# A TensorE-bound kernel in 66 steps: a new instruction list, an output half cut in two, and one weight piece fewer kept in memory

## The chip, the cores and the metric

One NeuronCore of a Trainium2 chip. The metric is the device time of one execution, in microseconds (us), median of the runs. The kernel before takes 3138.72 us (three runs, 3137.41 to 3142.72). The same kernel differs between chips (3133.5 to 3142.3 us for the kernel before, medians of five sets of runs; the later four are from chips 15, 8, 14 and 10), so an experiment is always compared with runs of the kernel before on its own chip.

## The reference

```python
def _A_ref(x, mem0, Wq, Wk, Wv, Wo, seg_len):      # 64 segments of 32 rows, 32 heads of 192
    ...
    for s in range(n_seg):
        xs = x[:, s * seg_len:(s + 1) * seg_len, :].copy()
        h = jnp.concatenate([mem, xs], axis=1)           # 8 memory rows + 32 rows
        q = jnp.einsum('btd,dhe->bhte', h, Wq)           # k and v alike
        ...
        o = jnp.einsum('bhte,hed->btd', o, Wo)
        mem = o[:, :M, :].copy()                         # the next segment needs this one
        outs.append(o[:, M:, :])
def _B_ref(x, wqkv, wo):  # local dilated attention, 32 heads of 20
    ...
x = A_x
x = x + _A_ref(_layernorm(x), A_mem0, A_Wq, A_Wk, A_Wv, A_Wo, A_seg_len)
x = x + _B_ref(_layernorm(x), B_wqkv, B_wo)
x = x + _A_ref(_layernorm(x), A_mem0, A_Wq, A_Wk, A_Wv, A_Wo, A_seg_len)   # same weights again
x = x + _B_ref(_layernorm(x), B_wqkv, B_wo)
```

(Defaults cut.) The width is 640, and layer A's projections are 640 x 6144, so A's weights are 31.5 MB; the kernel keeps only a part of them on the core. The memory rows make layer A a recurrence over 64 segments.

## The kernel before

The kernel runs a segment of the first layer pair and a segment of the second, two segments behind, as two lanes of 40 columns in the same matmuls. That makes 66 steps for A; 62 of them have both lanes (I call them full steps), the first two and the last two have one. After the last there is one more step of B alone.

In each step all of A's weights are used once. They are cut into 128 pieces of eight or seven 128x128 blocks ("long", 256 KB, and "short", 224 KB). Some pieces are resident (loaded once and kept in the core's memory); the others are streamed in every step through a ring of eight slots:

```python
RING = 8
N_RES = 79
PIECE = (8, 7)
...
def load_piece(self, u):
    ...
    res = u in self.resident
    if res:
        t_ = self.wres.tile([P, w], BF16, name="w_{}{}_{}{}".format(*u))
    else:
        t_ = self.wring.tile([P, P * PIECE[0]], BF16, name="w_ring")
    ...
    self.nc.sync.dma_start(out=t_[:, 0:w], in_=src)
```

The order of all instructions of a step is one hand-set list. Heads are handled in eight "quads". For quad i, Ki, Qi, Vi are projections (30 matmuls each); KEi, QEi, VEi copy them out of PSUM, the memory that matmuls write to (KE, VE on ScalarE, QE on VectorE); Ti, TEi transpose V and copy it; Si are the scores, Ei the exponentials (ScalarE), EMi the mask (VectorE); POi is probabilities times V; Ri the reciprocal of the sums (three ScalarE instructions); OT1i, OT2i the normalised outputs (VectorE, three instructions); Oai, Obi the two halves of the output projection, 15 matmuls each. LSQ, lst, LMV, LR, LAP are the layer norm of the next step, MEMa and MEMb copy the new memory rows into the next step's input, X1 adds the residual. Small letters are layer B. The end of the list before:

```
... OT24 VE6 Ob1 E6 QE7 PO5 T6 EM6 TE6 by byE R5 K7 KE7 V7 S7 VE7 OT15 E7 OT25 LSQ PO6 EM7 Oa2 R6 T7 Ob2 Oa3 TE7
Ob3 OT16 OT26 Oa5 PO7 Oa6 R7 lst LMV Ob5 Oa4 Ob6 OT17 LR OT27 Ob4 LAP O7x O7y MEMa O7z MEMb X1
```

Each engine gets its own instructions in this order, and the timelines below show them in it. There is one buffer for PO's result, so PO7 waits for OT26.

The softmax here doesn't subtract the row's maximum and nothing guards it: scores larger than these inputs give would overflow.

Of the kernel before, what the change touches and what calls it, by code (L numbers as in the profile page):

```python
# [21 lines left out]
NQUAD = 8  # L22
# [13 lines left out]
BDIL = 2  # L36

RING = 8
N_RES = 79
PIECE = (8, 7)  # L40
O_ROWS = ((0, 2, 3), (5, 1, 4))

# [2 lines left out]


ORDER = """
K0 Q0 bsq K0y QE0 KE0 V0 bst bmv VE0 Q1 S0 K1 T0 QE1 br bap E0 TE0 KE1 V1 S1 EM0 Q3 PO0 VE1 QE3 E1 bq T1 R0 K2
KE2 bqE TE1 Q2 K3 V2 QE2 OT10 S2 KE3 bk EM1 OT20 S3 PO1 VE2 E2 bkE Q4 T2 EM2 bs1 E3 QE4 V3 R1 K4 TE2 be1 VE3
Q5 OT11 OT21 KE4 PO2 R2 EM3 T3 eb1 bs0 be0 V4 QE5 Oa0 VE4 bv TE3 OT12 OT22 bvE Q6 S4 PO3 eb0 E4 bt R3 QE6 btE  # L50
K5 T4 EM4 K6 KE5 TE4 bp0 V5 OT13 Ob0 OT23 KE6 on0 S5 bp1 VE5 PO4 T5 Oa1 E5 R4 on1 TE5 V6 bo Q7 EM5 OT14 S6 boE
OT24 VE6 Ob1 E6 QE7 PO5 T6 EM6 TE6 by byE R5 K7 KE7 V7 S7 VE7 OT15 E7 OT25 LSQ PO6 EM7 Oa2 R6 T7 Ob2 Oa3 TE7
Ob3 OT16 OT26 Oa5 PO7 Oa6 R7 lst LMV Ob5 Oa4 Ob6 OT17 LR OT27 Ob4 LAP O7x O7y MEMa O7z MEMb X1
""".split()


# [4 lines left out]
def half_order():  # L61

    order = []
    for n in ORDER:
        if n[0] in "KQV" and len(n) == 2:
            order += [(n[0].lower(), int(n[1]), 0), (n[0].lower(), int(n[1]), 1)]
        elif n[:2] in ("Oa", "Ob"):
            order.append(("o", int(n[2]), int(n[1] == "b")))
        elif n == "O7x":
            order += [("o", 7, 0), ("o", 7, 1)]  # L70
    assert len(set(order)) == len(order) == 8 * NQUAD
    return order

def half_blocks(kind, i, h):

    if kind == "o":
        if i == NQUAD - 1:
            blocks = [(m, c) for c in range(NC) for m in O_ROWS[0] + O_ROWS[1]]
        else:
            blocks = [(m, c) for rows in O_ROWS for m in rows for c in range(NC)]  # L80
    elif (kind, i) == ("k", 0):
        blocks = [(c, n) for c in range(NC - 1) for n in range(6)] + [(NC - 1, n) for n in range(6)]
    else:
        blocks = [(c, n) for n in range(6) for c in range(NC)]
    return blocks[15 * h:15 * (h + 1)]


NO_WEIGHTS = {"T": 4, "S": 3, "PO": 3, "bst": 3, "lst": 3, "bq": 10, "bk": 10, "bv": 8, "bt": 3, "bo": 2, "by": 8, "bp": 2, "bs": 8}

def resident_pieces():  # L90

    at, t = {}, 0.0
    for n in ORDER:
        if n[0] in "KQV" and len(n) == 2 and n != "K0":
            at.update({(n[0].lower(), int(n[1]), h): t + 15 * h for h in range(2)})
        elif n == "K0":
            at.update({("k", 0, h): t + 15 * h for h in range(2)})
        elif n[:2] in ("Oa", "Ob"):
            at[("o", int(n[2]), int(n[1] == "b"))] = t
        elif n == "O7x":  # L100
            at.update({("o", 7, h): t + 15 * h for h in range(2)})
        t += 30 if len(n) == 2 and n[0] in "KQV" else 15 if n[0] == "O" and n[1] in "ab" else 30 if n == "O7x" else NO_WEIGHTS.get(n.rstrip("01234567"), 0)
    pieces = [(at[u] + 8 * q, u + (q,)) for u in half_order() for q in range(2)]
    pieces.sort()
    stream, n_s = set(), len(pieces) - N_RES
    k = 0
    for j in range(n_s):
        want = (j + 0.5) * t / n_s
        while k < len(pieces) - (n_s - j) and abs(pieces[k + 1][0] - want) <= abs(pieces[k][0] - want):
            k += 1  # L110
        stream.add(pieces[k][1])
        k += 1
    return {u for _, u in pieces} - stream

class Kernel:
    def __init__(self, ctx, tc, xT, m0T, wA, wqkv, wo, out):

        self.tc = tc
        self.nc = tc.nc
        self.x = xT  # L120
        self.mem0 = m0T
        self.wA = wA
        self.b_src = (wqkv, wo)
        self.out = out
        self.n_seg = 2 * xT.shape[0]
        pool = lambda name, bufs, **kw: ctx.enter_context(tc.tile_pool(name=name, bufs=bufs, **kw))
        self.cp = pool("consts", 1)
        self.wres = pool("wres", 1)
        self.wring = pool("wring", RING)
        self.ap1 = pool("act1", 1)  # L130
        self.ap2 = pool("act2", 2)
        self.bp = pool("bact", 1)
        self.xp = pool("xio", 1)
        self.ps_one = pool("ps_one", 1, space=PSUM)
        self.units = {}
        self.place = {u: n for n, u in enumerate(half_order())}
        self.resident = resident_pieces()
        self.cur = {}
        self.n_big = 0
        self.xt, self.ots, self.qxs, self.kp, self.qp, self.vp, self.tp = {}, {}, {}, {}, {}, {}, {}  # L140
        self.x_load(0)
        self.build_consts()
# [154 lines left out]
    def proj(self, ps, kind, i, h, t, chained=False):  # L297

        hT = self.hT[t % 2]
        c0, c1 = self.cs.start, self.cs.stop  # L300
        for k, (c, n) in enumerate(half_blocks(kind, i, h)):
            yield k
            self.nc.tensor.matmul(ps[:, NT * n + c0:NT * n + c1], lhsT=self.block(kind, i, h, k), rhs=hT[:, NT * c + c0:NT * c + c1],  # L303
                                  start=(h == 0 and k == 0) if chained else c == 0, stop=(c == NC - 1), skip_group_check=chained)
# [111 lines left out]
    def o_mm(self, i, h, k, first=False):  # L416
        m, c = half_blocks("o", i, h)[k]
        ot = self.ots[i][:].rearrange("p a b n -> p (a b) n")
        o = NT * (c % 3) + self.cs.start
        self.nc.tensor.matmul(self.acc[c // 3][:, o:o + self.cs.stop - self.cs.start], lhsT=self.block("o", i, h, k), rhs=ot[:, m, self.cs],  # L420
                              start=first, stop=False, skip_group_check=True)
# [8 lines left out]
    def a_o7(self, part):  # L430

        for k in {"x": range(18), "y": range(18, 24), "z": range(24, 30)}[part]:
            self.o_mm(NQUAD - 1, k // 15, k % 15)

    def acc_lanes(self, g):

        return self.acc[g][:, 0:(3 - g) * NT].rearrange("p (c l n) -> p c l n", l=2, n=LT)
# [301 lines left out]
    def a_piece(self, n, t):  # L739
        if n == "K0":  # L740
            return self.k0(t)
        if n == "K0y":
            return self.k0y()
        if n[:2] == "O7":
            return self.a_o7(n[2])
        if n == "X1":
            return self.b_x1(t)
        k, i = n[:-1], int(n[-1])
        if k == "K":
            self.kp[i] = self.proj6("k", i, t)  # L750
        elif k == "Q":
            self.qp[i] = self.proj6("q", i, t)
        elif k == "V":
            self.vp[i] = self.proj6("v", i, t)
        elif k in ("Oa", "Ob"):
            self.a_o(i, int(k == "Ob"))
        else:
            {"KE": self.kE, "QE": self.qE, "VE": self.vE, "T": self.a_t, "TE": self.tE, "S": self.a_s, "E": self.sE, "EM": self.sM,
             "R": self.dR, "PO": self.a_pv, "OT1": self.ot1, "OT2": self.ot2}[k](i)
# [51 lines left out]
def laid_out(A_x, A_mem0, A_Wq, A_Wk, A_Wv, A_Wo, B_wqkv, B_wo):  # L811

    chunks = lambda a: a.reshape(a.shape[0], NC, P, -1).transpose(0, 2, 1, 3).reshape(a.shape[0], P, -1)
    x = A_x[0]
    xT = x.reshape(x.shape[0] // NX, NX, D).transpose(0, 2, 1)
    w = {k: a.reshape(D, NQUAD, QE).transpose(1, 0, 2) for k, a in (("k", A_Wk), ("q", A_Wq), ("v", A_Wv))}
    w["o"] = A_Wo.reshape(NQUAD, QE, D)

    def half(k, i, h):
        b = w[k][i].reshape(-1, P, w[k].shape[2] // P, P)  # L820
        b = np.stack([b[r, :, c] for r, c in half_blocks(k, i, h)], 1)
        return np.concatenate([b[:, :PIECE[0]].ravel(), b[:, PIECE[0]:].ravel()])

    wA = np.stack([half(*u) for u in half_order()])
    wo = B_wo.reshape(BH // 2, 2, BD, D).transpose(1, 0, 2, 3).reshape(2, D // 2, D)
    wo = np.stack([wo[0, 0:P], wo[1, 192:], wo[0, P:256], wo[1, 64:192], np.concatenate([wo[0, 256:], wo[1, 0:64]])], 1).reshape(P, -1)
    out = {"xT": chunks(xT), "m0T": chunks(A_mem0[0].T[None])[0], "wA": wA, "wqkv": chunks(B_wqkv.reshape(D, 3, D).transpose(1, 0, 2)), "wo": wo}
    return {k: np.ascontiguousarray(v) for k, v in out.items()}
# [24 lines left out]
```

## Time and profile before

| | before |
|---|---|
| median | 3138.72 us |
| TensorE busy | 98% of the span |
| bound of a full step by its matmuls alone, my estimate from their start-to-start times | 46.2 us |
| undisturbed full step (the shortest of 62) | 46.43 us |
| mean full step | 46.62 us |
| streamed per step | 49 pieces, 11,808 KB |

From the page of the kernel before: the busy times; two lines of its DMA queues (packets, MB, share of 16 engines); and the engines' shares of the chain that ended last (the waits followed back from the last instruction of the kernel).

```profile
PE 3063.2 (98%) x83160; PEld 3036.4 (97%) x83160; DVE 2358.2 (75%) x6883; ACT 1747.2 (56%) x3829; POOL 48.2 (2%) x162
...
q1 hardware_dynamic: 477648, 820.89, 83.2%
q8 instruction: 651, 10.67, 1.4%
...
PE 95%; DMA 3%; issue 1%; DVE 1%; ACT 0%; SPq 0%; DVEq 0%; ACTq 0%
```

TensorE (PE), with 95% of that chain, is the bound: everything else matters only where it makes TensorE wait, or sets when it may go on. The second queue: 651 packets of 16,384 B. TensorE has 83,160 weight loads and as many matmuls, 166,320 instructions; with the 475 others of its trace that is 651 blocks of 256, so I take these packets for TensorE's own instructions. The profile counts them on the same 16 DMA engines as the weights (1.4% of the span, the weights' queue 83.2%).

What fills a full step is best read from the starts of matmuls. In this trace a pair of weight load and 80-column matmul takes 35.7 ns, a 128-column one 56 ns, start to start. The following lines are from the timeline of TensorE in the kernel before, in the last 9 us of a full step; columns are start, duration, engine, line, operation, tiles, shape, count. The lines are, in order: end of V7, PO6, PO7, the last seven blocks of the output projection, and the first blocks of K0 of the next step.

```profile
1529.37 0.42 PE L303 MATMUL ps_v<-hT_92,w_v_11_1654 128*128 128x80 bf16 x7
...
1529.90 0.45 PE L401 MATMUL ps_o<-Em,Vt_134 80*128 80x80 bf16 x8
...
1533.25 0.46 PE L401 MATMUL ps_o<-Em,Vt_134 80*128 80x80 bf16 x8
...
1537.17 0.42 PE L420 MATMUL ps_acc_51496<-OT,w_o_11_1962 128*128 128x80 bf16 x7
1537.61 0.45 PE L303 MATMUL ps_k<-hT_90,w_k_00_386 128*128 128x80 bf16 x8
```

A group of seven issues in 7 x 35.7 = 250 ns (the printed duration contains the modelled end of the last one). So the last group is issued by 1537.42, and K0 starts at 1537.61: TensorE waits 0.19 us. That is the "hand-over" wait, found in nearly every full step. Before PO7 there is another, 0.035 us. What it waits for is the timeline of ScalarE (ACT) and VectorE (DVE) of the same stretch:

```profile
1529.83 0.56 ACT L342 CAST VT_140<-ps_v 128x480 bf16<-128x480 f32 x1 [0.52 <-PE ps_v L303]
1530.28 0.43 ACT L374 ACTIVATE Em<-ps_s 80x320 bf16<-80x320 f32 x1
1530.74 0.88 ACT L388 ACTIVATE R<-ps_o 64x320 f32<-64x320 f32 x2
1531.65 0.47 ACT L390 ACTIVATE R<-R 128x320 f32<-128x320 f32 x1
1533.80 0.88 ACT L388 ACTIVATE R<-ps_o 64x320 f32<-64x320 f32 x2 [1.68 <-PE ps_o L401]
1534.71 0.47 ACT L390 ACTIVATE R<-R 128x320 f32<-128x320 f32 x1
```

```profile
1535.21 0.49 DVE L408 TENSOR_TENSOR OT<-ps_o,R 128x320 bf16<-128x320 f32 x1
...
1536.29 0.49 DVE L500 TENSOR_TENSOR ln_xc<-xin_86,ln_m 128x320 f32<-128x320 bf16 x1
1536.88 0.56 DVE L502 TENSOR_TENSOR hT_90<-ln_xc,ln_r 128x160 bf16<-128x160 f32 x2
1537.36 0.20 DVE L454 CAST hT_90<-ps_acc_51495 128x48 bf16<-128x48 f32 x1
```

PO7 starts at 1533.25 and issues for 0.285 us; R7 on ScalarE starts 0.26 us after that; then the three OT products, the layer-norm apply, and the copy of the memory rows follow one another on VectorE with almost no gap, and K0 follows the copy. From the end of PO7 to K0 it is a chain of 4.08 us. TensorE has other work for 3.86 us of it; the rest is the hand-over wait.

There is a third kind of loss, "issue" in the profile: matmuls that wait for no semaphore and still start late. In full steps they are rare and irregular (0.16 us per step in this profile). In the two last, one-lane steps they are regular; from the timeline of TensorE there:

```profile
3040.20 0.28 PE L303 MATMUL ps_v<-hT_90,w_ring 128*128 128x40 bf16 x5
3041.27 0.20 PE L303 MATMUL ps_v<-hT_90,w_ring 128*128 128x40 bf16 x2 [0.80 <-issue]
...
3045.00 0.20 PE L303 MATMUL ps_k<-hT_90,w_k_01_1016 128*128 128x40 bf16 x2
3045.95 0.29 PE L303 MATMUL ps_k<-hT_90,w_k_01_1016 128*128 128x40 bf16 x5 [0.74 <-issue]
```

From one such wait to the next are exactly 128 pairs, which are 256 instructions. Two instruction packets of the second queue ended at 3040.02 and 3044.67 us, 1.25 and 1.28 us before the matmuls that went on. So I read them as late instruction fetches.

### The profile page before, as it was taken

The page shows a single profiled execution, that of the slowest core. Times are in us where ns is not written, and L with a number is a line of the kernel's source. Part 1 is how long each engine was busy: PE and PEld are TensorE (multiplying, and loading weights), DVE is VectorE, ACT ScalarE, POOL GpSimd, SP SyncE. Part 2 cuts the span into 40 slices and gives each one's busy share as a digit, 9 for nine tenths or more (in the row PEclk, how much of TensorE's full clock was granted, in tenths as well). Part 3 has the DMA queues.
Part 4 walks back from the last instruction along what each step waited for, and adds up shares of the span by engine and source line. Part 5 has one row for each costly group of instructions (what it writes and reads, how often), then busy time and mean ns, then how long its engine had stood idle before and what let it go on. Part 6 is the DMA issues. An engine that isn't in the chain of part 4 may idle for free.

```text
span 3138.8 us, 185804 instructions
## 1 busy us (share of the span) xinstructions
PE 3063.2 (98%) x83160; PEld 3036.4 (97%) x83160; DVE 2358.2 (75%) x6883; ACT 1747.2 (56%) x3829; POOL 48.2 (2%) x162
## 2 busy tenths in 40 slices
PE   6899999999999999999999999999999999999996
PEld 5799999999999999999999999999999999999996
DVE  3577777777777777777777777777777777777775
ACT  2355556555556556556555655555655655655653
POOL 2000000000000000000000000000000000000000
PEclk6899999999999999999999999999999999999998
DMA  9988888888888888888888888888888888888885
GB/s 360 320 263 267 263 262 265 264 264 265 266 268 263 268 266 263 268 266 263 268 266 261 267 263 267 261 265 268 263 267 266 264 267 267 263 269 266 262 274 184
DMA packets 487807, 838.02 MB, mean 267 GB/s; under 512 B 54240, under 2 KB 261984, under 8 KB 487008
## 3 DMA queue, kind: packets, MB, share of 16 engines
q1 hardware_dynamic: 477648, 820.89, 83.2%
q8 instruction: 651, 10.67, 1.4%
q10 hardware_dynamic: 9360, 5.26, 0.6%
q14 instruction: 148, 1.21, 0.1%
HBM read 823.31 MB, written 2.62 MB: 263 GB/s over the span
## 4 chain that ended last, share of the span: by engine, by line
PE 95%; DMA 3%; issue 1%; DVE 1%; ACT 0%; SPq 0%; DVEq 0%; ACTq 0%
PE ps_k L303 18%; PE ps_q L303 18%; PE ps_v L303 18%; PE ps_vt L349 6%; PE ps_o L401 5%; PE ps_s L368 5%; PE ps_by L634 2%; PE ps_bq L523 2%; PE ps_bv L548 2%; PE ps_bk L523 2%; DMA w_ring<-in_wA_dram 1%; PE ps_bs L575 1%; PE ps_bo L598 1%; PE ps_bvt L561 1%; PE ps_st L473 0%
## 5 line engine op out<-in xcount | busy, mean ns | idle before, releaser
L303 PEld LDWEIGHTS <-w_ring 128*128 128x128 bf16 x17754 | 784.4, 100 | 19.4 <-DMA w_ring<-in_wA_dram 10.5
L388 ACT ACTIVATE R<-ps_o 64x320 f32<-64x320 f32 (+1 forms) x1056 | 448.5, 425 | 273.8 <-PE ps_o L401 223.6
L342 ACT CAST VT_140<-ps_v 128x480 bf16<-128x480 f32 (+1 forms) x528 | 288.9, 547 | 230.7 <-PE ps_v L303 227.6
L329 ACT CAST KF_121<-ps_k 128x480 bf16<-128x480 f32 (+1 forms) x264 | 144.1, 546 | 391.2 <-PE ps_k L303 383.3
L374 ACT ACTIVATE Em<-ps_s 80x320 bf16<-80x320 f32 (+1 forms) x528 | 223.3, 423 | 157.2 <-PE ps_s L368 110.7
L420 PEld LDWEIGHTS <-w_ring 128*128 128x128 bf16 x6600 | 291.2, 100 | 3.5 <-DMA w_ring<-in_wA_dram 2.6
L335 DVE CAST QT_127<-ps_q 128x320 bf16<-128x320 f32 (+1 forms) x264 | 127.1, 481 | 203.4 <-PE ps_q L303 203.4
L357 DVE COPY Vt_134<-ps_vt 80x512 bf16<-80x512 bf16 x528 | 219.2, 415 | 71.5 <-PE ps_vt L349 69.3
L349 PE MATMUL ps_vt<-ident,VT_140 128*128 128x128 bf16 x3168 | 267.7, 221 | 0.0
L408 DVE TENSOR_TENSOR OT<-ps_o,R 128x320 bf16<-128x320 f32 (+1 forms) x528 | 249.9, 473 | 22.3 <-ACT R L390 16.6
L329 ACT CAST KF_123<-ps_k 128x480 bf16<-128x480 f32 (+1 forms) x264 | 144.1, 546 | 205.6 <-PE ps_k L303 203.9
L390 ACT ACTIVATE R<-R 128x320 f32<-128x320 f32 (+1 forms) x528 | 244.0, 462 | 16.6
L401 PE MATMUL ps_o<-Em,Vt_134 80*128 80x80 bf16 (+1 forms) x4224 | 238.0, 199 | 1.4 <-issue 1.3
L335 DVE CAST QT_125<-ps_q 128x320 bf16<-128x320 f32 (+1 forms) x264 | 126.5, 479 | 143.1 <-PE ps_q L303 71.9
L349 PEld LDWEIGHTS <-VT_140 128*128 128x128 bf16 x3168 | 191.5, 99 | 0.1
L303 PE MATMUL ps_q<-hT_92,w_ring 128*128 128x80 bf16 (+1 forms) x3234 | 185.8, 201 | 3.7 <-DMA w_ring<-in_wA_dram 2.6
L303 PE MATMUL ps_q<-hT_90,w_ring 128*128 128x80 bf16 (+1 forms) x3234 | 186.3, 201 | 2.2 <-DMA w_ring<-in_wA_dram 1.5
L401 PEld LDWEIGHTS <-Vt_134 80*128 80x128 bf16 x4224 | 181.6, 98 | 1.0 <-issue 0.7
L303 PE MATMUL ps_k<-hT_90,w_ring 128*128 128x80 bf16 (+1 forms) x3003 | 172.7, 201 | 1.4 <-DMA w_ring<-in_wA_dram 0.7
L303 PE MATMUL ps_k<-hT_92,w_ring 128*128 128x80 bf16 (+1 forms) x3003 | 171.8, 201 | 1.4 <-issue 1.4
L380 DVE TENSOR_TENSOR Em<-Em,maskA 80x320 bf16<-80x320 bf16 (+1 forms) x528 | 163.2, 309 | 12.5 <-ACT Em L374 8.4
L414 DVE TENSOR_TENSOR OT<-ps_o,R 64x160 bf16<-64x160 f32 (+1 forms) x528 | 165.1, 313 | 7.3
(3084 smaller groups left out, 8305.2 us busy)
## 6 DMA issues: line engine op xcount, KB each, us to landing
w_ring<-in_wA_dram SPq DMA_DIRECT2D x1716, 256.0 KB, 3.9
w_ring<-in_wA_dram SPq DMA_DIRECT2D x1518, 224.0 KB, 4.0
out_dram<-YT_94 ACTq DMA_DIRECT2D x32, 80.0 KB, 3.7
wqkv_sb<-in_wqkv_dram SPq DMA_DIRECT2D x3, 800.0 KB, 7.7
wo_sb<-in_wo_dram SPq DMA_DIRECT2D x1, 800.0 KB, 7.4
w_k_00_386<-in_wA_dram SPq DMA_DIRECT2D x1, 256.0 KB, 2.8
w_k_10_405<-in_wA_dram SPq DMA_DIRECT2D x1, 256.0 KB, 3.8
w_q_10_438<-in_wA_dram SPq DMA_DIRECT2D x1, 256.0 KB, 4.6
```

What stands on the lines that cost most here:

```text
L303: self.nc.tensor.matmul(ps[:, NT * n + c0:NT * n + c1], lhsT=self.block(kind, i, h, k), rhs=hT[:, NT * c + c0:NT * c + c1], start=(h == 0 ...
L329: self.nc.scalar.copy(out=kf[:, :, self.cs], in_=self.kp[i][:, 0:6 * NT].rearrange("p (a n) -> p a n", a=6)[:, :, self.cs])
L335: nc.vector.tensor_copy(out=qt[:, :, 0:4:3, cs], in_=pv[:, :, 0:3:2, cs])
L342: self.nc.scalar.copy(out=vt[:, :, self.cs], in_=self.vp[i][:, 0:6 * NT].rearrange("p (a n) -> p a n", a=6)[:, :, self.cs])
L349: nc.tensor.transpose(out=ps[:, n, :], in_=self.VT[:, NT * n:NT * n + P], identity=self.ident[:])
L357: nc.vector.tensor_copy(out=vt[:, :, 0:4:3, :], in_=src[:, :, 0:3:2, :])
L374: self.nc.scalar.activation(out=e[0:NT, :, cs], in_=self.sv[i][0:NT, :, cs], func=ACT.Exp, scale=float(DH) ** -0.5)
L388: self.nc.scalar.activation(out=r[rows, :, :, self.cs], in_=d, func=ACT.Ln)
L390: self.nc.scalar.activation(out=rf, in_=rf, func=ACT.Exp, scale=-1.0)
L401: nc.tensor.matmul(ov[:, pr, b, self.cs], lhsT=vt[0:NT, 512 * pr + P * b:512 * pr + P * (b + 1)], rhs=em[0:NT, 2 * pr + b // 2, self.cs], ...
L408: self.nc.vector.tensor_tensor(out=ot[:, :, 0:3:2, cs], in0=self.ov[:, :, 0:4:3, cs], in1=self.r[i][:, :, :, cs], op=ALU.mult)
L420: self.nc.tensor.matmul(self.acc[c // 3][:, o:o + self.cs.stop - self.cs.start], lhsT=self.block("o", i, h, k), rhs=ot[:, m, self.cs], sta ...
```

## The change

Its words: the last output chunks of the seventh quad's half go behind the eighth quad's first chunks; the list comes from a model of the schedule in which the layer-norm sums take as long as in the trace. The diff, cut to its core (the bookkeeping for the new names O6x and O6y is left out):

```diff
-N_RES = 79
+N_RES = 78
 ORDER = """
-K0 Q0 bsq K0y QE0 KE0 V0 bst bmv VE0 Q1 S0 K1 T0 QE1 br bap E0 TE0 KE1 V1 S1 EM0 Q3 PO0 VE1 QE3 E1 bq T1 R0 K2
 ... (four lines cut; the whole list is new)
-OT24 VE6 Ob1 E6 QE7 PO5 T6 EM6 TE6 by byE R5 K7 KE7 V7 S7 VE7 OT15 E7 OT25 LSQ PO6 EM7 Oa2 R6 T7 Ob2 Oa3 TE7
-Ob3 OT16 OT26 Oa5 PO7 Oa6 R7 lst LMV Ob5 Oa4 Ob6 OT17 LR OT27 Ob4 LAP O7x O7y MEMa O7z MEMb X1
+K0 K0y K1 KE0 Q0 bsq V0 KE1 QE0 bst Q1 S0 bmv VE0 QE1 T0 TE0 br V1 E0 EM0 S1 bap Q2 E1 QE2 VE1 EM1 K2 PO0 KE2
+... (four lines cut)
+VE6 EM5 boE EM6 Q7 QE7 PO5 T6 R5 by TE6 Ob1 K7 V7 byE KE7 OT15 OT25 LSQ VE7 PO6 R6 Oa2 T7 Ob2 TE7 S7 Oa5 E7
+OT16 OT26 lst Oa6 O6x EM7 PO7 Oa3 LMV Ob3 R7 OT17 Oa4 Ob5 LR O6y OT27 Ob4 O7x LAP MEMa O7y O7z MEMb X1
 """
 ...
             blocks = [(m, c) for rows in O_ROWS for m in rows for c in range(NC)]
+            if i == NQUAD - 2:
+                blocks = blocks[:15] + sorted(blocks[15:], key=lambda b: b[1])
 ...
+    def a_o6(self, part):
+
+        for k in {"x": range(9), "y": range(9, 15)}[part]:
+            self.o_mm(NQUAD - 2, 1, k)
```

O6x is the first nine matmuls of the half that was Ob6, O6y the last six. The number of resident pieces falls to 78: which pieces are resident follows from the list, and 79 of the new list would be 43 long and 36 short ones (38 and 41 before), too much by 256 B per partition. With 78 the core streams 50 pieces, 12,064 KB per step, 2.2% more than before.

More of the change, by code (lines that the diff above doesn't have):

```diff
@@ L47 @@
 ORDER = """
-K0 Q0 bsq K0y QE0 KE0 V0 bst bmv VE0 Q1 S0 K1 T0 QE1 br bap E0 TE0 KE1 V1 S1 EM0 Q3 PO0 VE1 QE3 E1 bq T1 R0 K2
-KE2 bqE TE1 Q2 K3 V2 QE2 OT10 S2 KE3 bk EM1 OT20 S3 PO1 VE2 E2 bkE Q4 T2 EM2 bs1 E3 QE4 V3 R1 K4 TE2 be1 VE3
-Q5 OT11 OT21 KE4 PO2 R2 EM3 T3 eb1 bs0 be0 V4 QE5 Oa0 VE4 bv TE3 OT12 OT22 bvE Q6 S4 PO3 eb0 E4 bt R3 QE6 btE
-K5 T4 EM4 K6 KE5 TE4 bp0 V5 OT13 Ob0 OT23 KE6 on0 S5 bp1 VE5 PO4 T5 Oa1 E5 R4 on1 TE5 V6 bo Q7 EM5 OT14 S6 boE
-OT24 VE6 Ob1 E6 QE7 PO5 T6 EM6 TE6 by byE R5 K7 KE7 V7 S7 VE7 OT15 E7 OT25 LSQ PO6 EM7 Oa2 R6 T7 Ob2 Oa3 TE7
-Ob3 OT16 OT26 Oa5 PO7 Oa6 R7 lst LMV Ob5 Oa4 Ob6 OT17 LR OT27 Ob4 LAP O7x O7y MEMa O7z MEMb X1
+K0 K0y K1 KE0 Q0 bsq V0 KE1 QE0 bst Q1 S0 bmv VE0 QE1 T0 TE0 br V1 E0 EM0 S1 bap Q2 E1 QE2 VE1 EM1 K2 PO0 KE2
+T1 TE1 R0 bk S2 bkE Q3 OT10 V2 Q4 E2 VE2 OT20 PO1 T2 QE3 QE4 TE2 V3 R1 K3 VE3 KE3 EM2 bq Oa0 S3 OT11 OT21 bqE
+PO2 E3 T3 TE3 R2 Q5 bs0 K4 bv QE5 be0 EM3 KE4 OT12 OT22 bs1 eb0 bvE be1 V4 bt S4 PO3 btE Q6 VE4 K6 E4 R3 eb1
+EM4 QE6 KE6 V5 T4 OT13 bp0 VE5 OT23 TE4 K5 bp1 PO4 T5 on0 KE5 Ob0 on1 S5 V6 R4 E5 TE5 OT14 OT24 S6 Oa1 E6 bo
+VE6 EM5 boE EM6 Q7 QE7 PO5 T6 R5 by TE6 Ob1 K7 V7 byE KE7 OT15 OT25 LSQ VE7 PO6 R6 Oa2 T7 Ob2 TE7 S7 Oa5 E7
+OT16 OT26 lst Oa6 O6x EM7 PO7 Oa3 LMV Ob3 R7 OT17 Oa4 Ob5 LR O6y OT27 Ob4 O7x LAP MEMa O7y O7z MEMb X1
 """.split()
@@ L68, in half_order @@
             order.append(("o", int(n[2]), int(n[1] == "b")))
+        elif n == "O6x":
+            order.append(("o", 6, 1))
         elif n == "O7x":
@@ L99, in resident_pieces @@
             at[("o", int(n[2]), int(n[1] == "b"))] = t
+        elif n == "O6x":
+            at[("o", 6, 1)] = t
         elif n == "O7x":
             at.update({("o", 7, h): t + 15 * h for h in range(2)})
-        t += 30 if len(n) == 2 and n[0] in "KQV" else 15 if n[0] == "O" and n[1] in "ab" else 30 if n == "O7x" else NO_WEIGHTS.get(n.rstrip("01234567"), 0)
+        t += 30 if len(n) == 2 and n[0] in "KQV" else 15 if n[0] == "O" and n[1] in "ab" else 30 if n == "O7x" else 15 if n == "O6x" else NO_WEIGHTS.get(n.rstrip("01234567"), 0)
     pieces = [(at[u] + 8 * q, u + (q,)) for u in half_order() for q in range(2)]
@@ L743, in a_piece @@
             return self.k0y()
-        if n[:2] == "O7":
-            return self.a_o7(n[2])
+        if n[:2] in ("O6", "O7"):
+            return self.a_o7(n[2]) if n[1] == "7" else self.a_o6(n[2])
         if n == "X1":
```

## The prediction

> **What bounds the kernel.** TensorE. The busy table has PE at 98%, the chain of waits 95%; granted clock 1.0 after the start. The program is 66 steps of 1260 weight-load/matmul pairs. Reading matmul starts in the timeline, an 80-column pair takes 35.7 ns, a full step 46.43 us at best, about 46.6 on average. My estimate from these start-to-start times: the matmuls alone fill 46.2 us. What is left per full step:
> - hand-over to the next step (last output block to first key block): 0.19 us, in almost every step;
> - the wait of the eighth attention product (PO7): 0.035 us;
> - irregular stalls averaging 0.16 us, mostly "issue". In the two last, half-lane steps they come every 4.5 us, one per 128 pairs, like the 16 KB packets of the queue of kind "instruction". [...] here a full step consumes one in about 4.7 us, hardly above 4.5, so sometimes it is not hidden.
>
> So perfect steps would gain about 62 x 0.39 = 24 us, 0.8%.
>
> **What the change does.** No instruction is added or removed. The list is reordered; the second half of the seventh quad's output is cut 9+6 with its 15 blocks sorted by column; one weight piece fewer is resident (78), so 50 instead of 49 are streamed per step, 12,064 KB for 11,808 (+2.2%; DMA share 0.855 to about 0.875). Despite the words, the cut-off six stand before the eighth's first chunks.
>
> **The hand-over.** The timeline shows the chain from PO7's end: ScalarE starts R7 after 0.26 us, three activations (0.433, 0.433, 0.470), three OT products on VectorE (1.05 together), layer-norm apply (1.1), copy of the memory rows (0.20), next step: 4.08 us in all. TensorE had 105 blocks and the statistics pair to do meanwhile (3.86 us); after, 111 blocks, 3.96 us. The gap should fall from 0.19 to about 0.11 us: 62 x 0.08 = 5 us won.
>
> **PO6 to PO7.** R6 now precedes E7 on ScalarE (E7 delayed it by 0.4 us). But this stretch is tight: adding durations along VectorE (sums 2.15, vector-transpose copy 0.61, OT 1.05, mask 0.31), OT16 ends when Oa6 wants it, OT26 when O6x wants it, EM7 about 0.03 us after PO7 could start; T7 comes 0.82 us after V7 and its copy needs about 0.8. I expect 0.02 to 0.1 us of stall instead of 0.035. Elsewhere I find 0.3 us or more.
>
> **DMA.** The ring runs seven pieces ahead (6.5 us, landing takes 4), so no steady starvation. Slightly more irregular stalls (+1 to 3 us); step 1 wants second-layer key weights earlier.
>
> **Sum.** -5 +1 (tight stretch) +2 = about -2.5 us.
>
> Predicted: 3136 us, range 3129 to 3144. Chances: faster by over 2% 0.01, within 2% 0.97, slower by over 2% 0.02.
>
> **Right or wrong would show as:** hand-over gap about 0.11 us; full-step minimum about 46.35 us; streamed transfers 50 per step, DMA share up 0.02; the irregular stalls a little larger; PO7, Oa6, O6x waits under 0.1 us together.
>
> **What would make it wrong.** VectorE late by more than I summed in the tight stretch, which shifts PO7 and all behind it one for one, 62 times; a wait in the reordered middle (bqE, be1/Q6, on0) that I judged slack; instruction fetches crossing from just hidden to just exposed under the extra DMA load, which could cost 0.1 us each, ten a step, 60 us.

The sum: -5 +1 +2, recorded as about -2.5 us. "One in about 4.7 us" is one 16 KB packet of the instruction queue; "not hidden" is my reading of the irregular stalls. The 0.1 us each in the last sentence was a guess, with no measurement behind it.

## The result, and the profile after

The changed kernel takes 3151.83 us (three runs, 3151.6 to 3152.07), 13 us more than before. A ratio here is the mean time of one kernel's fast runs over that of the other's in the same rounds, so it is not quite the ratio of the quoted medians: 1.0039, with a 95% interval of 1.0016 to 1.0062. The size of the effect lies well within 2%, but it has the other sign than predicted, and 3151.83 lies outside the predicted range of 3129 to 3144.

The page of the changed kernel, busy times and DMA queues as above (its chain of waits has the same shares, PE 95%):

```profile
PE 3071.2 (98%) x83160; PEld 3042.6 (97%) x83160; DVE 2385.2 (76%) x6883; ACT 1747.4 (55%) x3829; POOL 48.5 (2%) x162
...
q1 hardware_dynamic: 487008, 837.93, 84.1%
q8 instruction: 651, 10.67, 1.4%
```

Same instruction counts, 17 MB more data, same bound. The 62 full steps together, from the stretches of the trace (start and end, length, then busy time of PE, weight load, DVE, ACT, POOL, and granted clock, DMA share, GB/s), first before:

```profile
138.04:3028.21 2890.17, 2883.24 (x78120) 2872.88 (x78120) 2235.18 (x6448) 1667.62 (x3596) 25.22 (x61) 1.00 0.85 265
```

and after:

```profile
142.12:3039.46 2897.34, 2887.84 (x78120) 2875.73 (x78120) 2261.50 (x6448) 1667.45 (x3596) 25.31 (x61) 1.00 0.86 270
```

So of the 11.1 us between the two profiled spans (3149.9 and 3138.8), 7.2 us lie in the full steps. 4.1 us lie in the first two steps (132.9 us instead of 128.7), in which all the weights are loaded for the first time; the rest is -0.2 us. I took the full steps apart by comparing each matmul's start-to-start time with the usual one of its shape, and by asking whether the late matmul carries a semaphore wait:

| per full step, us | before | after |
|---|---|---|
| undisturbed step (shortest) | 46.432 | 46.454 |
| wait of Oa6's first block | none | 0.11 |
| wait of PO7 | 0.035 | 0.055 |
| hand-over to the next step | 0.19 | 0.09 |
| late matmuls that wait for no semaphore, mean | 0.16 | 0.22 |

The fixed waits sum to 0.255 instead of 0.225 us: the shorter hand-over is paid for in front of PO7. That part is 62 x 0.022 = 1.4 us. The larger part, 62 x 0.06 = 3.8 us, are the irregular stalls; about 2 us more are semaphore waits that come in one or two steps each. The timeline of TensorE after at the hand-over (last output blocks, first blocks of K0):

```profile
1588.67 0.42 PE L426 MATMUL ps_acc_53024<-OT,w_o_11_1963 128*128 128x80 bf16 x7
1589.02 0.45 PE L309 MATMUL ps_k<-hT_92,w_k_00_386 128*128 128x80 bf16 x8
```

The last group is issued by 1588.92, so K0 waits 0.10 us in this step.

The timeline of TensorE after, in the lines that answer to those above (end of V7, PO6, the first blocks of Oa6, PO7):

```profile
1580.74 0.42 PE L309 MATMUL ps_v<-hT_90,w_v_11_1653 128*128 128x80 bf16 x7
1581.00 0.46 PE L407 MATMUL ps_o<-Em,Vt_134 80*128 80x80 bf16 x8
...
1583.74 0.27 PE L426 MATMUL ps_acc_53023<-OT,w_o_00_1770 128*128 128x80 bf16 x3
...
1584.65 0.46 PE L407 MATMUL ps_o<-Em,Vt_134 80*128 80x80 bf16 x8
```

and the timeline of ScalarE after:

```profile
1581.20 0.56 ACT L348 CAST VT_140<-ps_v 128x480 bf16<-128x480 f32 x1 [0.52 <-PE ps_v L309]
1581.78 0.88 ACT L394 ACTIVATE R<-ps_o 64x320 f32<-64x320 f32 x2
1582.69 0.47 ACT L396 ACTIVATE R<-R 128x320 f32<-128x320 f32 x1
1583.19 0.43 ACT L380 ACTIVATE Em<-ps_s 80x320 bf16<-80x320 f32 x1
```

PO6 issues from 1581.00 to 1581.29. R6 could start 0.26 us later, at 1581.55. It starts at 1581.78, the moment the copy of V7 (VE7) is done. In the list before, E7 stood between VE7 and R6 and held R6 by about 0.3 us, but no wait of Oa6 came of it; in the new list E7 is behind R6, but PO6 now follows directly on V7, so VE7 is still in the way. OT16 follows R6, and Oa6 waits for OT16. The timeline of VectorE after shows that OT16 waited for R6 and not for VectorE, which had been idle for 0.21 us:

```profile
1583.20 0.49 DVE L414 TENSOR_TENSOR OT<-ps_o,R 128x320 bf16<-128x320 f32 x1 [0.21 <-ACT R L396]
```

### The profile page after: what moved, and what is told of

Its sections match the earlier page's. It is cut to its first block, busy times and chain, and to the rows that moved or that the text cites. A ratio compares the mean times of both kernels' runs of the same rounds, so it can differ in the third digit from the quotient of the medians.

```text
span 3149.9 us, 186002 instructions
## 1 busy us (share of the span) xinstructions
PE 3071.2 (98%) x83160; PEld 3042.6 (97%) x83160; DVE 2385.2 (76%) x6883; ACT 1747.4 (55%) x3829; POOL 48.5 (2%) x162
## 3 DMA queue, kind: packets, MB, share of 16 engines
q14 instruction: 149, 1.22, 0.1%
## 4 chain that ended last, share of the span: by engine, by line
PE 95%; DMA 3%; issue 1%; DVE 1%; ACT 0%; SPq 0%; DVEq 0%; ACTq 0%
PE ps_k L309 18%; PE ps_q L309 18%; PE ps_v L309 18%; PE ps_vt L355 6%; PE ps_o L407 5%; PE ps_s L374 5%; PE ps_bq L534 2%; PE ps_by L645 2%; PE ps_bk L534 2%; PE ps_bv L559 2%; PE ps_bs L586 1%; DMA w_ring<-in_wA_dram 1%; PE ps_bo L609 1%; PE ps_bvt L572 1%; PE ps_st L484 0%
## 5 line engine op out<-in xcount | busy, mean ns | idle before, releaser
L309 PEld LDWEIGHTS <-w_ring 128*128 128x128 bf16 x17952 | 793.9, 100 | 22.1 <-DMA w_ring<-in_wA_dram 15.6
L426 PEld LDWEIGHTS <-w_ring 128*128 128x128 bf16 x6930 | 300.9, 100 | 7.6 <-issue 4.2
L309 PE MATMUL ps_v<-hT_90,w_ring 128*128 128x80 bf16 (+1 forms) x3003 | 172.5, 201 | 4.5 <-DMA w_ring<-in_wA_dram 3.5
L309 PE MATMUL ps_q<-hT_92,w_ring 128*128 128x80 bf16 (+1 forms) x3003 | 172.1, 201 | 4.9 <-DMA w_ring<-in_wA_dram 4.1
L309 PE MATMUL ps_q<-hT_90,w_ring 128*128 128x80 bf16 (+1 forms) x3003 | 172.8, 201 | 2.6 <-DMA w_ring<-in_wA_dram 2.1
L309 PE MATMUL ps_v<-hT_92,w_ring 128*128 128x80 bf16 (+1 forms) x3003 | 171.9, 201 | 2.5 <-issue 2.4
L309 PE MATMUL ps_k<-hT_90,w_ring 128*128 128x80 bf16 (+1 forms) x2970 | 171.1, 201 | 2.1 <-DMA w_ring<-in_wA_dram 1.6
```

What stands on the lines that cost most here:

```text
L309: self.nc.tensor.matmul(ps[:, NT * n + c0:NT * n + c1], lhsT=self.block(kind, i, h, k), rhs=hT[:, NT * c + c0:NT * c + c1], start=(h == 0 ...
L426: self.nc.tensor.matmul(self.acc[c // 3][:, o:o + self.cs.stop - self.cs.start], lhsT=self.block("o", i, h, k), rhs=ot[:, m, self.cs], sta ...
```

## The experiments

Two theories about the 13 us: **the list** (the new order, and the tight stretch around PO6 in it), and **the streaming** (the 50th piece, whose bytes delay the instruction fetches). A third possible part, the first two steps, had to be told from chance. All times in this table are medians; each ratio is to the kernel before on the same chip.

| run | what | time, us | before there | ratio (95% interval) |
|---|---|---|---|---|
| a_rep | changed kernel again | 3142.11 | 3133.52 | 1.0030 (1.0018 to 1.0043) |
| b78 | before, 78 resident | 3145.82 | 3133.52 | 1.0032 (1.0019 to 1.0044) |
| a79s | changed, 79 resident | 3133.82 | 3133.52 | 1.0000 (0.9987 to 1.0012) |
| a_ob1 | changed, Ob1 moved | 3253.36 | 3133.52 | 1.0376 (1.0362 to 1.0390) |
| b_rep | before again | 3135.45 | 3134.84 | 0.9999 (0.9987 to 1.0011) |
| b_dummy | before, 224 KB added | 3138.93 | 3134.84 | 1.0016 (1.0004 to 1.0028) |
| a_ob1b | Ob1 moved, 5 OT buffers | 3132.09 | 3134.84 | 0.9993 (0.9981 to 1.0006) |
| b_r7 | before, ring 7, 80 resident | 3135.44 | 3134.84 | 0.9998 (0.9987 to 1.0010) |
| best2 | a_ob1b with 79 resident | 3128.33 | 3135.20 | 0.9979 (0.9967 to 0.9991) |
| best1 | a_ob1b, ring 7, 80 resident | 3126.68 | 3135.20 | 0.9969 (0.9957 to 0.9981) |
| a_unsplit | changed, O6 in one piece | 3149.63 | 3135.20 | 1.0040 (1.0028 to 1.0052) |
| a_o6late | changed, O6y after O7x | 3144.59 (one run) | 3135.20 | none |
| b78_2 | b78 again | 3153.49 | 3142.31 | 1.0038 (1.0026 to 1.0050) |
| b_dummy_2 | b_dummy again | 3150.62 | 3142.31 | 1.0029 (1.0017 to 1.0041) |
| b_dose4 | before, 4 x 224 KB added | 3177.36 | 3142.31 | 1.0111 (1.0097 to 1.0126) |

All were correct.

### a_rep: the changed kernel again

No edit.

> The changed kernel once more, as the yardstick for the others of this set. The slowdown against before (about 13 us) has, in the two profiles so far, three parts: +4.1 us in steps 0 and 1 (first loading of all weights), +1.9 us in the fixed waits of a full step (46.46 instead of 46.43 us for an undisturbed one, 62 times), +5.3 us in irregular stalls of the full steps. If the start-up part belongs to the list, steps 0 and 1 together take 132.9 us again, within 1 us; if it was chance of that one profile, they come nearer the 128.7 us of before. Fixed waits must repeat to 0.01 us per step whichever theory holds.

Measured: ratio 1.0030; fixed waits 0.11, 0.055, 0.09 us again, undisturbed step 46.454 us. The first two steps took 129.9 us, not 132.9. Over all profiles, these two steps took 128.7 to 132.9 us with the list before (seven profiles, the one with four added transfers left out) and 129.9 to 133.4 us with the changed list and its relatives (nine), so the 4.1 us of the first comparison are not shown to belong to the list. The irregular stalls vary as well from profile to profile (0.13 us per step here, 0.22 in the first); for those, the timed runs have to decide.

### b78: only the residency

```diff
-N_RES = 79
+N_RES = 78
```

> The kernel before with 78 resident pieces instead of 79 and nothing else, so 50 streamed per step (12,032 KB instead of 11,808). Streaming theory: the extra transfer slows the instruction fetches and the first loading, so most of the slowdown is here already: irregular stalls up by 3 to 6 us over the full steps, 3144 to 3149 us. List theory (the stalls come of the new order, not of the bytes): within 2 us of before. The fixed waits stay 0.19 and 0.035 us per step in both.

Measured: ratio 1.0032, about 10 us. That is as much as the whole change, with the list untouched. The undisturbed step stays 46.435 us. The streaming theory holds; the list theory's "within 2 us of before" is refused.

### a79s: the changed list without the 50th piece

```diff
-N_RES = 78
+N_RES = 79
 ...
-    return {u for _, u in pieces} - stream
+    kept = {u for _, u in pieces} - stream
+    return (kept - {("q", 0, 1, 0)}) | {("q", 0, 1, 1)}
```

> The changed list with 79 resident pieces (one long piece exchanged for its short sister so that it fits in memory), 49 streamed per step, 11,680 KB, a little less even than before. Streaming theory: 5 to 9 us faster than the changed kernel, 3143 to 3147 us, with irregular stalls back at about 0.16 us per full step. List theory: within 2 us of the changed kernel. The fixed waits stay 0.11, 0.055 and 0.09 us in both.

Measured: 8.3 us faster than the changed kernel on the same chip, equal to before (1.0000). The fixed waits are those of the changed list. Irregular stalls fell to 0.05 us per step, lower than expected. So the new list by itself is neutral within the 4 us of the interval, and the loss came with the 50th piece. (This run streams 11,680 KB, 1% less than before, so it may flatter the list slightly.)

### a_ob1: a repair of the tight stretch that forgot a buffer

```diff
-PO5 T6 R5 by TE6 Ob1 K7 V7 byE KE7 OT15 OT25 LSQ VE7 PO6 R6
+PO5 T6 R5 by TE6 K7 V7 Ob1 byE KE7 OT15 OT25 LSQ VE7 PO6 R6
```

> The changed list with Ob1 (15 output matmuls, 0.54 us) moved from before K7 to between V7 and PO6. ScalarE-queue theory: in the changed kernel the copy of V7 stands before R6 on ScalarE and holds it 0.2 us; with Ob1 between them R6 starts 0.26 us after the end of PO6 instead of 0.5, the waits of Oa6 (0.11) and PO7 (0.055) fall below 0.03 and 0.04 us, an undisturbed full step takes about 46.32 us, and the time falls by about 9 us against the changed kernel of this set. VectorE-queue theory (the layer-norm sums and the transpose copy of T7 hold OT16, not R6): OT16 comes no earlier, the waits stay, less than 3 us gained.

Measured: 3253 us, 110 us slower than the changed kernel; neither theory expected that. The waits of TensorE in a_ob1 over about four full steps (who waited for whom: us in total, times, longest):

```profile
PE ps_o L407 <- DVE OT L420: 4.8, 4, 1.2
PE ps_acc L426 <- DVE OT L414: 1.2, 4, 0.3
```

PO6 waits for OT25 in every step. Quad 5's OT lies in the same one of four buffers as quad 1's, which Ob1 reads; moving Ob1 back by 60 matmuls moved OT15 behind it, and OT25, which must free PO's buffer before PO6, with it. The experiment said nothing about the two theories; it showed only that a move on TensorE moves a VectorE write behind it.

### a_ob1b: the same with a fifth OT buffer

```diff
 (as a_ob1, and)
-tag=f"OT{i % 4}"
+tag=f"OT{i % 5}"
```

> The moved Ob1 once more, with five OT buffers instead of four, so that the OT of quad 5 no longer has to wait until Ob1 has read the buffer of quad 1 (that wait cost 1.4 us per step in the first attempt). 78 resident pieces and 12,064 KB streamed, as in the changed kernel. ScalarE-queue theory: R6 starts 0.26 us after PO6, the waits of Oa6 and PO7 nearly vanish, an undisturbed full step takes 46.30 to 46.35 us instead of 46.46, 7 to 10 us faster than the changed kernel (that was 1.003 of before), so 0.9995 to 1.0010 of before. VectorE-queue theory: waits stay, 1.002 to 1.004 of before.

Measured: undisturbed step 46.286 us (expected 46.30 to 46.35), ratio 0.9993 at the bytes of the changed kernel. The timelines of TensorE (end of V7, PO6, PO7) and of ScalarE (VE7, R6) in a_ob1b:

```profile
1572.82 0.63 PE L309 MATMUL ps_v<-hT,w_v 128*128 128x80 bf16 x13
...
1573.83 0.46 PE L407 MATMUL ps_o<-Em,Vt 80*128 80x80 bf16 x8
...
1577.32 0.45 PE L407 MATMUL ps_o<-Em,Vt 80*128 80x80 bf16 x8
```

```profile
1573.49 0.56 ACT L348 CAST VT<-ps_v 128x480 bf16<-128x480 f32 x1 [0.52 <-PE ps_v L309]
1574.37 0.88 ACT L394 ACTIVATE R<-ps_o 64x320 f32<-64x320 f32 x2 [0.32 <-PE ps_o L407]
```

VE7 now ends at 1574.05, ScalarE idles 0.32 us, and R6 starts 0.26 us after the end of PO6 (1573.83 + 0.285). From PO6 to PO7 it is 3.49 us instead of 3.65, and the waits of Oa6 and PO7 are gone; the hand-over wait stays 0.09. From V7 to PO6 TensorE now has 15 more matmuls to do, which gives ScalarE the time for VE7; what VectorE has to do between PO5 and PO6 is unchanged. So VE7 in front of R6 was what made the stretch tight. (The fifth OT buffer was changed together with the move; it was not run alone.)

### a_unsplit: what the cut of the half is worth

```diff
-OT16 OT26 lst Oa6 O6x EM7 PO7 Oa3 LMV Ob3 R7 OT17 Oa4 Ob5 LR O6y OT27 Ob4 O7x ...
+OT16 OT26 lst Oa6 Ob6 EM7 PO7 Oa3 LMV Ob3 R7 OT17 Oa4 Ob5 LR OT27 Ob4 O7x ...
```

> The changed kernel with the last half of the seventh quad's output in one piece again, in front of PO7 (all 15 blocks where the changed list has 9, the other six taken from before Ob4). Chain theory (from PO7 on the step ends a fixed time later): the wait of PO7 (0.055 us) vanishes, PO7 runs 0.16 us later, the hand-over wait grows from 0.09 to about 0.30 us, an undisturbed full step takes 46.61 to 46.63 us instead of 46.46 and the time rises by about 10 us against the changed kernel: ratio 1.005 to 1.008 of before. If the split is worth nothing: 46.46 us and ratio about 1.003.

Measured: undisturbed step 46.609 us and hand-over wait 0.304 us, both as the chain theory said; the wait of PO7 is gone. The timed ratio is 1.0040, below the expected 1.005 to 1.008; the increase over the changed kernel (1.0030 and 1.0039 in other sets of runs) is not resolved across chips, but in the trace the split is worth 0.155 us per step.

### a_o6late: the six blocks where the change's words put them

```diff
-... LR O6y OT27 Ob4 O7x LAP MEMa ...
+... LR OT27 Ob4 O7x O6y LAP MEMa ...
```

> The changed kernel with the cut-off six blocks really behind the eighth quad's first chunks (after O7x instead of before Ob4), as the change's name says. Chain theory: the hand-over waits for VectorE (layer-norm apply, then the memory copy), not for O7x, so nothing changes: hand-over 0.09 us, undisturbed full step 46.46 us within 0.01. If the copy of the memory rows waits for O7x on TensorE, it starts earlier and the hand-over wait falls below 0.05 us.

Measured (one look): hand-over 0.09 us, undisturbed step 46.456 us. It makes no difference, because the hand-over is set by VectorE's chain behind PO7, not by the end of O7x.

### b_rep: the kernel before, profiled again

No edit.

> The kernel before itself, as the yardstick and for a profile on this chip. A ratio of 1.000 within 0.0015. Irregular stalls (matmuls that wait for no semaphore and start late) between 0.05 and 0.2 us per full step, every one of them ending 1.2 to 1.6 us after the end of a 16 KB packet of the instruction queue; fixed waits 0.19 and 0.035 us.

Measured: ratio 0.9999. The fixed waits were 0.195 and 0.038 us, the irregular stalls 0.08 us per step in this profile. I looked at each matmul of the full steps that carries no semaphore wait and starts over 60 ns late, and at the instruction packet that ended last before it, in this profile and all others:

| profile | added or removed per step against before | such stalls | sum, us | they end after a packet's end by, us |
|---|---|---|---|---|
| before | | 36 | 9.9 | 1.18 to 1.55 |
| b_rep | | 16 | 4.8 | 1.24 to 1.53 |
| a79s | -128 KB | 11 | 3.0 | 1.27 to 1.51 |
| b78, b78_2 | +224 KB | 29, 36 | 11.9, 13.7 | 1.22 to 1.62 |
| changed kernel, a_rep | +256 KB | 40, 20 | 13.7, 8.1 | 1.24 to 1.63 |
| b_dummy, b_dummy_2 | +224 KB | 18, 45 | 5.5, 15.1 | 1.22 to 1.61 |
| b_dose4 | +896 KB | 89 | 38.8 | 1.21 to 1.69 |

Packets come every 4.7 us, yet every single stall ends in a window half a microsecond wide, 1.2 to 1.7 us after one. A second count does not use these times at all. Number TensorE's instructions in the trace (weight loads, matmuls, and 410 to 540 others, mostly semaphore instructions) in blocks of 256. All of the some 470 such stalls in the full steps of all 17 profiles stand at the same place in a block, at instruction 192 or 193; none stands elsewhere. So I take the stalls for late instruction fetches. In the kernel before, 36 of 612 block boundaries in the full steps stalled. The packet that ended last before a boundary's matmul did so 2.3 us before it in the median (2.6 in b_rep, 2.0 in b_dose4 below).

So 576 of the 612 boundaries passed without a stall, with about 1 us to spare in the median (my estimate: the 2.3 us, less the 1.2 us at which stalls show). In the one-lane steps of the kernel before, where 128 pairs without their stall took 3.3 to 3.9 us, packets ended every 4.56 us on average (means of 4.4 to 4.7 us in the 17 profiles), and TensorE stalled 18 times; a full step consumes a block of 128 pairs in 4.7 us.

### b_dummy: the bytes without the piece

```diff
+            if n == "QE4" and a and t >= 3:
+                self.nc.scalar.dma_start(out=self.wo[:].rearrange("p m n -> p (m n)")[:, 0:896], in_=self.b_src[1][:, 0:896])
```

> The kernel before, its list and its 79 resident pieces untouched, with one added transfer per step: 224 KB in rows of 1,792 B, the same data written again over a third of the second layer's output weights, issued from ScalarE's queue where nothing waits for it. It adds the bytes of the 50th piece without adding a piece to the ring. Contention theory (more bytes delay the instruction fetches): slower than before by 5 to 12 us, irregular stalls up as in the run with 78 resident pieces. Ring theory (it is the 50th piece in the ring that hurts, by shortening the look-ahead): within 2 us of before.

Measured: ratio 1.0016, interval 1.0004 to 1.0028: between the two expectations, so not decided. Hence the repetition on one chip below.

### b_r7: fewer bytes, shorter look-ahead

```diff
-RING = 8
-N_RES = 79
+RING = 7
+N_RES = 80
```

> The kernel before with a ring of 7 slots instead of 8, the freed memory used for 80 resident pieces: 48 streamed per step, 11,520 KB (2.4% fewer than before), and only six pieces (about 5.8 us) of look-ahead against 4 us of landing. Contention theory: irregular stalls nearly vanish (below 0.06 us per step), 6 to 10 us faster than before. Look-ahead theory: semaphore waits at ring pieces appear (over 0.1 us per step) and the time is equal or worse.

Measured: 0.9998. Neither theory's size: the irregular stalls were 0.06 us per step, about as in b_rep on the same chip (0.08), so on this chip there was little left to win, and waits at ring pieces came to about 0.03 us per step. Going below the bytes of before gained nothing measurable there; going above cost 1.0016 (b_dummy, same chip).

### b78_2, b_dummy_2, b_dose4: bytes against the ring, on one chip

b78_2 and b_dummy_2 are b78 and b_dummy unchanged. b_dose4:

```diff
+            if n in ("QE1", "QE2", "QE4", "QE5") and a and t >= 3:
+                o = 896 * ("QE1", "QE2", "QE4", "QE5").index(n) % 2688
+                self.nc.scalar.dma_start(out=self.wo[:].rearrange("p m n -> p (m n)")[:, o:o + 896], in_=self.b_src[1][:, o:o + 896])
```

> The kernel before with 78 resident pieces (50 streamed, 224 KB more per step), again, on the chip of the next two. Bytes alone: the same ratio as the kernel with the added transfer of 224 KB, within 0.0012. Piece in the ring besides the bytes: 0.0015 or more above it. About 1.003 expected.

> The kernel before with an added transfer of 224 KB per step outside the ring, again, on the same chip. Bytes alone: 1.002 to 1.003 of before, equal to the run with 78 resident pieces within 0.0012. Ring: 1.000 to 1.0015.

> The kernel before with four added transfers of 224 KB per step outside the ring (896 KB, 7.6% more bytes). Contention theory: irregular stalls, again all ending 1.2 to 1.6 us after an instruction packet, grow to 0.3 to 0.8 us per full step, and the kernel is 20 to 50 us slower: ratio 1.006 to 1.016. If bytes do not matter to the fetches: ratio below 1.003 and stalls as in before. Semaphore waits at ring pieces over 0.2 us per step would mean that the weights themselves come late.

Measured: 1.0038 with the 50th piece, 1.0029 with the same bytes outside the ring, 1.0111 with four times the bytes. The first two agree within the 0.0012 set beforehand: the bytes explain most of the loss. In both pairs, here and on the earlier chips (1.0032 and 1.0016), the version with the piece in the ring was the slower one, so a smaller part of the ring's own is not excluded. The added transfer has rows of 1,792 B, as a short piece has; bytes and number of packets rose together and were not separated. The dose grows nearly in proportion, 0.0029 to 0.0111. From the waits of TensorE in the full steps of b_dose4:

```profile
PE ps_k L303 <- issue: 9.6, 19, 1.2
PE ps_v L303 <- issue: 5.7, 12, 1.3
PE ps_q L303 <- issue: 4.3, 7, 1.1
```

and the same view of the kernel before:

```profile
PE ps_q L303 <- issue: 0.8, 4, 0.2
PE ps_acc_62868 L420 <- issue: 0.6, 1, 0.6
```

The weights were hardly late in b_dose4: waits at ring pieces came to 0.05 us per full step, against 0.66 us of late matmuls that wait for no semaphore. By the reading above, TensorE waited for instructions. The fixed waits stayed at 0.19 and 0.035 us, so issuing the transfers on ScalarE did not hold up the chain. The transfers were issued from ScalarE's queue, not from the one that feeds the ring, and still cost 1.0016 and 1.0029. What the bytes do to a fetch is not shown to the end: once started, an instruction packet takes 0.96 to 0.97 us (median) in every one of these runs, so the delay should lie before its start. The trace agrees: in b_dose4 the packets before stalls started 2.5 us (median) after the first matmul of the block before, the other packets 1.5 us, and both took 0.97 us. The trace does not show when a fetch is asked for, so why they start late stays open.

### best2 and best1: both repairs together

```diff
 (best2: as a_ob1b, and)
-N_RES = 78
+N_RES = 79
-    return {u for _, u in pieces} - stream
+    kept = {u for _, u in pieces} - stream
+    swap = (("q", 0, 1), ("q", 2, 1), ("v", 3, 1), ("k", 5, 0), ("q", 7, 0))
+    return (kept - {u + (0,) for u in swap}) | {u + (1,) for u in swap}
 (best1: as a_ob1b, and)
-RING = 8
-N_RES = 78
+RING = 7
+N_RES = 80
```

> The two repairs together: moved Ob1 with five OT buffers, and 79 resident pieces (five long ones exchanged for their short sisters to fit), so 49 streamed per step and 11,808 KB, exactly the bytes of before, ring of 8. If the list repair (0.17 us per step less than the changed list, 0.15 less than before) and the streaming repair add up, an undisturbed full step takes 46.29 us, irregular stalls are at the level of before, and the kernel is 6 to 11 us faster than before: ratio 0.9965 to 0.998. If a faster step only exposes more instruction fetches (less slack per 128 pairs), the gain is under 4 us.

> The same list repair with a ring of 7 and 80 resident pieces: 48 streamed per step, 11,552 KB. Bytes theory (fewer bytes, fewer late fetches): a little faster than the other of this pair, ratio 0.996 to 0.9975. Look-ahead theory: the 0.03 to 0.04 us per step of ring waits that the ring of 7 showed earlier eat it up, ratio 0.997 to 0.999.

Measured: 0.9979 and 0.9969; both beat the kernel before on the same chip; the changed kernel did not run there, but stood at 1.0030 and 1.0039 elsewhere. The undisturbed step is 46.288 and 46.287 us. The ring waits of best1, which the look-ahead theory feared, came to 0.004 us per step. The two intervals overlap, so which of the two is better is not settled, though best1's five runs (3123.78 to 3126.98 us) all lie below best2's (3128.17 to 3130.39) on the same chip. The list of best1 gains 0.145 us per step, 62 x 0.145 = 9 us, and its time is 8.5 us below before.

## Why the prediction was wrong

- **"TensorE is the bound; perfect steps would gain about 24 us."** Right. TensorE is busy for 95% of the chain of waits before and after, and the best version found gained 8.5 us.
- **"The hand-over gap should fall from 0.19 to about 0.11 us, 5 us won."** Right in mechanism and nearly in size: 0.09 us, and the chain of 4.08 us behind PO7 is confirmed by a_unsplit and a_o6late.
- **"PO6 to PO7: 0.02 to 0.1 us of stall instead of 0.035."** Wrong in size: 0.11 + 0.055 = 0.165 us. The sum ran along VectorE and left out that ScalarE still had VE7 to do until 0.49 us after PO6, where R6 could have started at 0.26. The same sentence has T7 wait for V7's copy, but does not put that copy in front of R6. a_ob1b, which gives VE7 its time, removes both waits. So the sum of list effects was not the predicted -4 us but +1.4 us (46.454 against 46.432).
- **"Slightly more irregular stalls (+1 to 3 us)."** This is the step that failed most: the cost of the 50th piece. The mechanism, late instruction fetches, was named, but its term in the sum, +2 us, was too small by 8 to 10 us. 224 KB more per step cost 1.0032 and 1.0038 with nothing else changed, about 10 to 12 us, and 1.0016 and 1.0029 outside the ring. I had named the risk (fetches going "from just hidden to just exposed") and had seen the narrow margin (4.7 against about 4.5 us), but gave +1 to 3 us without a working, and the alternative, 60 us (ten fetches a step, as the trace has them, at a guessed 0.1 us each), as a mere risk; how many boundaries lay near the edge was not asked.
- **"The full-step minimum about 46.35 us; DMA share up 0.02."** 46.45 us; the share in the full steps rose from 0.85 to 0.86 as printed. The streamed pieces were 50 per step as said.
- **"Elsewhere I find 0.3 us or more of slack."** Right: no fixed wait appeared in the reordered middle in any profile.
- The prediction's sum was -2.5 us; the two mis-sized terms, about 5 us in the fixed waits (+1.4 instead of -4) and about 8 us in the bytes, turn it into about +11 us, against the measured 13 (ratio 1.0039) and 9 (1.0030).

Open: why the changed kernel lost 13 us on the first chip and 9 on the second (the intervals of the ratios overlap), why the fetches start later when more is moved, and whether the ring piece adds anything to its bytes.

## What to carry to other kernels

In this kernel TensorE's instructions came, as I read the traces, as a DMA stream of their own (651 packets of 16,384 B), and the matmuls that stalled on it carried no semaphore wait. Packets came every 4.4 to 4.7 us in the one-lane steps, where TensorE was held up by them, and a full step used up a block in 4.7 us. With so little to spare, 224 KB more per step cost 1.0016 to 1.0038 and 896 KB 1.0111, though waits at ring pieces came to only 0.05 us per step with the 896 KB. So in another kernel with a long unrolled stream of short matmuls, look for this: a matmul without a semaphore wait that starts late, here always 1.2 to 1.7 us after a packet of the instruction queue had ended. Before costing a reordering, add up every engine's queue on the chain, with all that stands in front of the link (here VE7 held R6 by 0.23 us), and check which buffer a moved read keeps occupied (a_ob1 lost 110 us to it). And look at what a new list does to derived settings: here 256 B per partition took one resident piece, and that decided the result.
